# Segment 0 of an infini-attention block: paired projection evictions, work moved to GpSimd, and a new timetable

## The chip, the cores and the metric

The kernel runs on one core of one Trainium2 chip. The metric is device time in microseconds of one execution. A core has five engines with a queue each, worked off strictly in order: TensorE (PE; its weight loads are listed as PEld), VectorE (DVE), ScalarE (ACT), GpSimd (POOL) and SyncE (SP), which here issues nearly all DMAs. Engines wait for one another by semaphores.

## The reference

One sequence of 2048 tokens of 576 channels in bf16, 32 heads of 18 channels, four segments of 512 tokens.

```
x = A_x
h = x + attention(layernorm(x)) @ wo
out = h + gelu(layernorm(h) @ w1 + b1) @ w2 + b2        # 4608 hidden channels

# attention, per head, segments s = 0..3, M = 0, z = 0 at first
a_dot = softmax(qs @ ks.T * scale + mask) @ vs           # within the segment
a_mem = (phi(qs) @ M) / (phi(qs) @ z + 1e-06)            # from the segments before
o     = g * a_mem + (1 - g) * a_dot                      # g = sigmoid(beta), one per head
M, z  = M + phi(ks).T @ vs,  z + sum(phi(ks))            # phi(t) = t + 1 if t > 0 else exp(t)
```

## The kernel before

**Stages.** `build()` describes the work as small operations of one engine each, by segment s: X (layernorm of x and its transpose), P (projections k, q, v), A (attention), M (update of the memory), B (output projection, residual h, second layernorm, transpose), C (first layer of the feed-forward part, F1, and gelu) and D (second layer, F2, and the output). Tokens are handled in tiles of 128 (tl = 0 to 3 in a segment).

**What sets the order.** `TIMETABLE` gives every operation a number and, where a row mixes letters, its engine (p TensorE, a ScalarE, d VectorE, g GpSimd, s SyncE). `schedule` (line 363) sorts all operations by that number and emits them in this order; so the numbers fix each engine's queue, and nothing else is reordered. The cost given to `add` (in us) does not change the order. It serves to pick buffers: `schedule` keeps an estimate of when each buffer of a `Slots` comes free and takes the one that is free first. A key is the stage's tag and the operation's name: `A01val` is the value products of segment 0, query tiles 0 and 1; the n-th entry of a row is the n-th such operation.

**Segment 0's path.** x comes in four tiles. For each, VectorE makes the statistics (`stats`: two BATCH_NORM_STATS2 and an aggregate, lines 669 and 670), GpSimd the reciprocal deviation (`rstd`, 673 and 674) and VectorE the scaled rows (`apply`, 684). Tiles 0 and 1 are only centred (`apply`, 682) and their deviation is multiplied in at the eviction. TensorE transposes (`TX`, 696), ScalarE or VectorE copies the result into xreg (594 or 598). Segments 1 to 3 store the rows and load them back with a transposing DMA (`flip`).

The projections of a tile are 2 x 5 matmuls of 288 columns, one bank of PSUM for each half of the channels. For q and k of tiles 0 and 1 both halves go into one tile of two banks (`proj2`, 750, pool `pr`) and one eviction takes both. All others (`proj`, 740) take one of four single banks `ps_c` for each half and have one eviction each (`copy`, 588). The keys' phi is made of three steps: `ek` (exp, ScalarE 821), `rk` (GpSimd 823) and `fk` (VectorE 825).

Tile 0's q and k are transposed by TensorE (`TQ`, 802), the other tiles' through DRAM (`qkst` and `A0flip`). Scores go into one tile of four banks (`st0`, 913), so each waits for the exp of the one before (ScalarE 916, 1.88 us). The diagonal blocks are masked on VectorE (926) or GpSimd (929), the value products (`val`, 945) are transposed back (`valT`, 959), divided and gated (`rec`, 963 and 964) and written (`comb`, 968).

**The memory.** `M` (849) sums phi(k).T v over the four tiles of a segment, in two halves of the heads. `macc` writes them to MZacc (859, copy in segment 0) or adds them (861). `mblk` (868) makes MZ_blk, the gated block-diagonal form, in four products on GpSimd; it needs MZ_blk zeroed (`memset`), the rows that carry the 1e-6 of the denominator (`eps`: 24 small memsets, 1320 to 1324) and the gates (`gmz`, 1358). Segment 1's `macc` may not change MZacc before segment 0's `mblk` has read it. `A1mem` (1041) is the first that multiplies with MZ_blk; it also needs phi(q) (`eg` ScalarE 1031, `rg` GpSimd 1033, `pq` VectorE 1035).

In segments 1 to 3 the local part of a head group is `valT` (1098), `rec2` (the reciprocal, 1102, and its product with the gate, 1103, both VectorE), `comb` (1106) and `comb2` (1109).

Of the kernel before, what the change touches and what calls it, by code (L numbers as in the profile page):

```python
# [11 lines left out]
ACT = mybir.ActivationFunctionType  # L12
# [12 lines left out]
    "A00exp": "a 89 106",  # L25
    "A00mask": "g 98 142 156 118",
    "A00st0": "p 82 101",
    "A01comb": "g 188 167 215 229",
    "A01exp": "a 124 140 160 176",
    "A01mask": "g136 d143 g180 g172",  # L30
    "A01oT": "d 228 233 230 236 235",
    "A01rec": "d 178 161 212 224",
    "A01st0": "p 119 137 155 170",
    "A01val": "p 149 200",
    "A01valT": "d 175 157 208 221",
    "A02comb": "g 294 347",
    "A02exp": "a 193 227 210 245 263 282 296",
    "A02mask": "g251 g238 g259 d309",
    "A02rec": "d 289 341",
    "A02st0": "p 189 223 207 242 260 276 291",  # L40
    "A02val": "p 255 279 313 315",
    "A02valT": "d 284 319",
    "A03comb": "g 408 449",
    "A03exp": "a 317 348 330 364 382 395 415",
    "A03mask": "g 353 365 370 428",
    "A03oT": "d 371 484 442 486 496",
    "A03rec": "d 386 445",
    "A03st0": "p 310 344 325 360 372 392 410",
    "A03val": "p 376 381 434 437",
    "A03valT": "d 385 440",  # L50
    "A0flip": "s 90 80 111 129 151 158 203 252",
    "A0opad": "g 127",
    "A1comb": "g534 g605 g630 g677 d714 g748 g790 d814",
    "A1comb2": "g541 g609 g636 g695 g731 g760 d798 d816",
    "A1eg": "a 390 377 472 542 650 680 683 741",
    "A1exp": "a 443 480 463 527 495 550 569 587 603 624 643 672 657 693 719 709 749 762 778 736",
    "A1flip": "s 352 340 414 477 520 516 615 645",
    "A1mask": "g444 g488 g492 g493 g497 g549 g526 d544 g563 g586 d600 g598 d631 g619 g641 g642 g674 g688 g697 g681 g664 g699 g725 d726 d769 d763 g768 d770 "
        "d774 g788 g764 g742",
    "A1mem": "p 458 471 606 607 662 735 708 756",  # L60
    "A1memT": "d 465 475 611 622 673 738 712 766",
    "A1memfin": "g538 g568 g625 g684 g723 d755 g751 g804",
    "A1oT": "d 678 707 782 819 821",
    "A1pq": "d 416 417 589 575 658 694 687 750",
    "A1rec": "d 467 482 621 676 706 739 718 785",
    "A1rec2": "d 532 579 628 675 713 743 789 812",
    "A1rg": "g 401 397 558 548 594 581 668 705",
    "A1st": "p 432 474 461 518 490 545 566 582 599 617 638 667 652 689 715 704 744 758 771 730",
    "A1val": "p 519 560 613 649 698 733 773 794",
    "A1valT": "d 530 573 623 654 711 740 779 807",  # L70
    "A2comb": "d931 d949 g983 g1014 g1053 d1072 g1126 d1157",
    "A2comb2": "g933 g964 g990 d1017 d1057 g1076 g1141 g1159",
    "A2eg": "a 732 837 903 935 948 956 1031 1055",
    "A2exp": "a 842 813 857 829 890 927 941 911 975 960 987 1011 1025 999 1045 1064 1074 1100 1087 1135",
    "A2flip": "s 671 783 808 864 850 889 1030 992",
    "A2mask": "d873 g862 g825 d868 g881 g855 g910 d908 g947 d950 d955 g958 d988 d986 g995 d982 d1028 d1027 g1020 d1033 g1032 g1006 d1050 g1049 g1094 g1079 "
        "d1109 g1106 g1131 d1095 g1146 d1147",
    "A2mem": "p 809 915 932 951 998 1009 1085 1078",
    "A2memT": "d 822 921 973 962 1001 1026 1090 1092",
    "A2memfin": "g909 g929 d977 g1010 d1021 g1060 g1133 g1128",  # L80
    "A2oT": "d 991 1052 1127 1165 1164",
    "A2pq": "d 800 904 928 945 994 1003 1062 1069",
    "A2rec": "d 866 926 976 969 1019 1043 1104 1102",
    "A2rec2": "d 901 943 981 1008 1047 1071 1124 1156",
    "A2rg": "g 754 878 916 937 874 952 1056 1065",
    "A2st": "p 839 797 853 826 875 923 938 905 972 953 984 1007 1022 997 1036 1058 1070 1096 1083 1120",
    "A2val": "p 877 919 970 996 1041 1063 1117 1151",
    "A2valT": "d 882 939 979 1005 1046 1068 1121 1155",
    "A3comb": "g1209 d1290 d1345 g1360 g1398 d1417 g1446 d1469",
    "A3comb2": "g1245 g1299 d1347 d1367 d1406 d1422 d1454 d1470",  # L90
    "A3eg": "a 1145 1178 1247 1304 1261 1337 1351 1396",
    "A3exp": "a 1152 1163 1171 1231 1184 1264 1277 1255 1309 1295 1344 1326 1357 1369 1389 1402 1412 1426 1440 1451",
    "A3flip": "s 1042 1093 1123 1099 1189 1276 1205 1334",
    "A3mask": "g1193 d1172 d1198 d1186 g1213 d1249 d1243 g1214 d1271 g1283 g1297 g1284 g1332 g1321 g1319 g1313 d1352 g1341 g1338 g1373 g1366 g1386 d1404 "
        "d1397 g1408 d1430 g1420 g1433 g1436 g1461 g1459 d1460",
    "A3mem": "p 1211 1268 1259 1343 1294 1361 1400 1414",
    "A3memT": "d 1217 1275 1280 1349 1305 1371 1415 1429",
    "A3memfin": "d1244 d1289 g1327 g1363 g1370 g1377 d1445 d1453",
    "A3oT": "d 1323 1424 1438 1474 1471",
    "A3pq": "d 1149 1215 1256 1317 1265 1340 1392 1401",  # L100
    "A3rec": "d 1234 1288 1285 1354 1328 1376 1427 1452",
    "A3rec2": "d 1206 1287 1324 1358 1395 1413 1444 1468",
    "A3rg": "g 1116 1114 1154 1310 1251 1308 1380 1383",
    "A3st": "p 1148 1160 1167 1197 1180 1262 1272 1252 1306 1292 1342 1322 1353 1365 1382 1399 1409 1421 1437 1447",
    "A3val": "p 1199 1260 1301 1339 1384 1407 1439 1462",
    "A3valT": "d 1203 1263 1316 1356 1394 1410 1443 1466",
    "B00Po": "p 244 248",
    "B00T": "p 299 307",
    "B00apply": "d 273",
    "B00copy": "d303 a312",  # L110
    "B00dma": "s 201 720",
    "B00hadd": "d 250 254",
    "B00rstd": "g 266",
    "B00stats": "d 256",
    "B00tail": "g 281",
    "B01Po": "p 262 267",
    "B01T": "p 301 308",
    "B01apply": "d 293",
    "B01copy": "d 305 314",
    "B01dma": "s 211 450",  # L120
    "B01hadd": "d 268 271",
    "B01rstd": "g 285",
    "B01stats": "d 277",
    "B01tail": "g 298",
    "B02Po": "p 503 523",
    "B02apply": "d 585",
    "B02dma": "s 452 793 592",
    "B02hadd": "d 508 528",
    "B02rstd": "g 571",
    "B02stats": "d 562",  # L130
    "B02tail": "g 590",
    "B03Po": "p 502 509",
    "B03apply": "d 543",
    "B03dma": "s 405 806 564",
    "B03flip": "s 635 626",
    "B03hadd": "d 512 514",
    "B03rstd": "g 522",
    "B03stats": "d 517",
    "B03tail": "g 556",
    "B1Po": "p 888 851 828 831 848 871 835 833",  # L140
    "B1apply": "d 918 860 900 856",
    "B1dma": "s 847 959 922 791 1139 887 838 954 912 792 849 865",
    "B1flip": "s 936 971",
    "B1hadd": "d 893 894 832 834 870 876 841 844",
    "B1rstd": "g 899 843 892 852",
    "B1stats": "d 896 836 884 846",
    "B1tail": "d920 d885 g906 d858",
    "B2Po": "p 1174 1176 1204 1216 1228 1223 1173 1170",
    "B2apply": "d 1229 1311 1278 1232",
    "B2dma": "s 1098 1238 1250 1182 1282 1318 1196 1431 1293 1091 1179 1237",  # L150
    "B2flip": "s 1336 1364",
    "B2hadd": "d 1183 1185 1208 1221 1239 1242 1175 1177",
    "B2rstd": "g 1226 1303 1273 1227",
    "B2stats": "d 1220 1225 1266 1187",
    "B2tail": "d1246 d1315 g1291 g1235",
    "B3Po": "p 1493 1490 1483 1481 1559 1561 1476 1479",
    "B3apply": "d 1549 1535 1570 1528",
    "B3dma": "s 1485 1498 1553 1423 1512 1540 1543 1618 1583 1428 1587 1531",
    "B3flip": "s 1593 1604",
    "B3hadd": "d 1495 1496 1488 1489 1560 1562 1480 1482",  # L160
    "B3rstd": "g 1548 1534 1568 1504",
    "B3stats": "d 1500 1497 1563 1484",
    "B3tail": "d1552 d1537 g1575 d1529",
    "C00F1": "p 329 318 346 383 366 413 446 438 481",
    "C00copy": "a336 d337 a327 d331 d363 d358 d407 d394 d375 d380 d424 d427 d460 d457 d447 d453 d491 d499",
    "C00dma": "s 173 217 261 326 335 359 374 398 423",
    "C00gelu": "a 422 505",
    "C01F1": "p 692 670 679 710 717 737 747 765 784",
    "C01copy": "d702 a701 d686 d685 d696 d691 d722 d721 a728 d729 d746 d753 d759 a757 d772 d786 d795 d803",
    "C01dma": "s 682 690 700 716 727 745",  # L170
    "C01gelu": "a 787 867",
# [1279 lines left out]
```

## Time and profile before

| what | us |
|---|---|
| three runs: median (lowest, highest) | 452.2 (448.96, 452.28) |
| the profiled execution | 450.67 |
| its span, first to last instruction | 449.0 |
| TensorE busy | 439.1 |
| VectorE busy | 292.0 |
| ScalarE busy | 298.9 |
| GpSimd busy | 180.2 |

The page gives each engine's busy time with its share of the span, the span in 40 slices (a digit is a share in tenths; PEclk is TensorE's granted clock in tenths of full speed), the chain of work that ended last, and groups of instructions by line. Other views list instructions in order of time (start, length, engine, line, output<-input), sum busy time by stretch, or say for whom an engine waited. A group's line reads: busy us, mean ns of one, then the engine's idle time before them and what ended it. TensorE's matmuls overlap, so its busy time also counts what a matmul needs to drain.

### The profile page before, as it was taken

The numbers are of one execution on the slowest core, as the hardware profiler recorded it, in microseconds if no ns is written. First come the engines' busy times: TensorE is split into PE (matmuls) and PEld (weight loads), VectorE is DVE, ScalarE is ACT, GpSimd is POOL, SyncE is SP. The second block draws the span as 40 slices with busy tenths as digits, with TensorE's granted clock in tenths as the row PEclk, the third lists the DMA queues.
The fourth block names the chain that finished last, engine by engine and source line by source line (L and its number), as shares of the span: only waits on it lengthen the run. The fifth ranks groups of instructions, "written<-read, shape, count | busy, mean of one in ns | idle before, by whom it ended". The sixth has DMA issues, their size and how long they took to land.

```text
span 449.0 us, 11498 instructions
## 1 busy us (share of the span) xinstructions
PE 439.1 (98%) x4815; PEld 280.3 (62%) x4815; DVE 292.0 (65%) x623; ACT 298.9 (67%) x267; POOL 180.2 (40%) x304
## 2 busy tenths in 40 slices
PE   8979999899999999999999999999999999999997
PEld 4756677566677677664344766645447875445775
DVE  6899896689888879887788877887675111000120
ACT  4879998799878879768899977674665002664000
POOL 6596667538874546744351437621201010000000
PEclk9989999899999999999999999999999999999999
DMA  7999989697788977874772925603552681640110
GB/s 267 235 236 251 255 212 293 195 251 234 181 214 279 295 252 177 234 110 117 199 214 77 216 88 130 142 36 108 154 175 73 169 241 24 213 161 1 39 42 26
DMA packets 81588, 76.54 MB, mean 170 GB/s; under 512 B 59008, under 2 KB 68736, under 8 KB 81536
## 3 DMA queue, kind: packets, MB, share of 16 engines
q1 hardware_dynamic: 81392, 75.66, 63.4%
q8 instruction: 37, 0.61, 0.5%
q10 hardware_dynamic: 144, 0.15, 0.1%
q14 instruction: 15, 0.12, 0.1%
HBM read 42.63 MB, written 19.20 MB: 138 GB/s over the span
## 4 chain that ended last, share of the span: by engine, by line
PE 92%; DVE 3%; POOL 2%; DMA 1%; issue 1%; ACT 0%; POOLq 0%
PE ps_c L1290 32%; PE ps_c L1203 16%; PE ps_c L747 16%; PE ps_l L1203 8%; PE ps_c L1240 7%; PE st L1064 4%; PE ps_c L1090 4%; PE ps_c L1041 1%; PE pr L758 1%; PE ps_c L849 1%; PE st L913 1%; DVE ln L669 1%; PE ps_c L945 1%; POOL MZ_blk L1324 1%; DMA x<-in_A_x_dram 1%
## 5 line engine op out<-in xcount | busy, mean ns | idle before, releaser
L1068 ACT ACTIVATE pt<-st 128x2048 bf16<-128x2048 f32 x60 | 112.6, 1877 | 34.9 <-PE st L1064 29.0
L1290 PEld LDWEIGHTS <-hT 128*128 128x128 bf16 x1152 | 110.7, 98 | 33.9 <-issue 5.7
L1203 PEld LDWEIGHTS <-w1g 64*128 64x128 bf16 x972 | 46.6, 94 | 56.5 <-issue 3.4
L1290 PE MATMUL ps_c<-w_lo,hT 128*128 128x288 bf16 x576 | 78.0, 286 | 0.0
L1290 PE MATMUL ps_c<-w,hT 128*128 128x288 bf16 x576 | 77.9, 286 | 0.0
L1203 PE MATMUL ps_c<-xreg,w1g 64*128 64x512 bf16 x648 | 72.9, 376 | 0.0
L747 PE MATMUL ps_c<-hT,xreg 128*128 128x288 bf16 (+1 forms) x440 | 62.6, 291 | 0.2
L1079 POOL TENSOR_SCALAR_AFFINE_SELECT pt<-pt 128x512 bf16<-128x512 bf16 x62 | 44.1, 720 | 44.7 <-ACT pt L1068 44.7
L1302 DVE TENSOR_TENSOR ot<-ps_c,hc 128x288 bf16<-128x288 f32 x32 | 14.1, 450 | 69.6 <-PE ps_c L1290 69.2
L1208 ACT ACTIVATE hT<-ps_l,b_col 128x512 bf16<-128x512 f32 x36 | 22.7, 685 | 46.8 <-PE ps_l L1203 46.8
L747 PEld LDWEIGHTS <-xreg 128*128 128x128 bf16 (+1 forms) x440 | 41.1, 99 | 15.9 <-issue 4.7
L1218 DVE TENSOR_SCALAR hT<-ps_c,b_col 128x512 bf16<-128x512 f32 x48 | 34.5, 743 | 13.8 <-PE ps_c L1203 13.6
L916 ACT ACTIVATE pt<-st 128x2048 bf16<-128x2048 f32 x20 | 37.6, 1879 | 3.2 <-PE st L913 2.4
L1240 PE MATMUL ps_c<-xreg,w1g 64*128 64x256 bf16 x648 | 38.1, 270 | 0.0
L1203 PE MATMUL ps_l<-xreg,w1g 64*128 64x512 bf16 x324 | 35.1, 376 | 0.0
L1240 PEld LDWEIGHTS <-w1g 64*128 64x128 bf16 x648 | 30.2, 94 | 6.7 <-issue 2.9
L673 POOL TENSOR_SCALAR ln<-ln 128x1 f32<-128x1 f32 x32 | 8.3, 259 | 64.4 <-DVE ln L670 62.5
L1223 ACT ACTIVATE hT<-hT 128x8192 bf16<-128x8192 bf16 (+2 forms) x6 | 31.8, 5321 | 0.3 <-DVE hT L1218 0.2
L1216 ACT ACTIVATE hT<-ps_c,b_col 128x512 bf16<-128x512 f32 x24 | 16.0, 685 | 16.3 <-PE ps_c L1203 16.1
L1064 PE MATMUL st<-qk 32*128 32x512 bf16 (+3 forms) x384 | 24.0, 303 | 0.0
L1251 DVE TENSOR_TENSOR hT<-ps_c,b_col 128x512 bf16<-128x512 f32 x31 | 20.6, 680 | 5.0 <-PE ps_c L1240 4.0
L747 PE MATMUL ps_c<-wt_o,oT 128*128 128x288 bf16 x160 | 22.5, 286 | 0.0
(111 smaller groups left out, 579.4 us busy)
## 6 DMA issues: line engine op xcount, KB each, us to landing
w1g<-in_B_w_dram SPq DMA_DIRECT2D x42, 576.0 KB, 4.9
qkd<-qk_pad SPq DMA_DIRECT2D x15, 512.0 KB, 3.8
hd<-h SPq DMA_DIRECT2D x16, 288.0 KB, 3.8
hc<-hd SPq DMA_DIRECT2D x16, 288.0 KB, 4.3
w_lo<-in_B_w_dram SPq DMA_DIRECT2D x3, 864.0 KB, 6.3
w<-in_B_w_dram SPq DMA_DIRECT2D x3, 864.0 KB, 9.7
xb<-in_A_x_dram SPq DMA_DIRECT2D x16, 144.0 KB, 4.2
x2d<-xn SPq DMA_DIRECT2D x14, 160.0 KB, 1.8
```

What stands on the lines that cost most here:

```text
L747: nc.tensor.matmul(out=c.t[:, 0:HALF], lhsT=xTb.t[0:kk, k, ts], rhs=wt[0:kk, hf, k, :], start=(k == 0), stop=(k == 4))
L916: ex = add(ps, {"act": 1.88}, lambda e: nc.scalar.activation(out=pt.t[:], in_=st.t[:], func=ACT.Exp, scale=scale), [sc], pt, [st], table=" ...
L1064: nc.tensor.matmul(out=st.t[:, i, off:off + n_], lhsT=qk[rows, 1, kt * P:(kt + 1) * P], rhs=qk[rows, 0, kt * P:L], start=True, stop=True, ...
L1068: ex = add(ps, {"act": 1.88}, lambda e, st=st, pt=pt: nc.scalar.activation(out=pt.t[:], in_=st.t[:], func=ACT.Exp, scale=scale), [sc], pt, ...
L1079: nc.gpsimd.affine_select(out=blk, in_=blk, pattern=[[0, 4], [1, P]], compare_op=ALU.is_ge, fill=0.0, base=0, channel_multiplier=-1)
L1203: nc.tensor.matmul(out=cc[w].t[:], lhsT=w1.t[rows, k, q, :], rhs=x2T[s].t[rows, k, :], start=(k == 0), stop=(k == ND - 1))
L1208: ready_f[f + w] = [add(pf - 12, {"act": 0.68}, lambda e, f=f, w=w, cc=cc: nc.scalar.activation(out=hT[:, :, f + w, :], in_=cc[w].t[:].rea ...
L1218: nc.vector.tensor_scalar(out=dst, in0=src, scalar1=b, scalar2=None, op0=ALU.add)
L1223: ge = add(2.9, {"act": 0.40 * (f1 - f0) + 0.25}, lambda e, f0=f0, f1=f1: nc.scalar.activation(out=hT[:, :, f0:f1, :], in_=hT[:, :, f0:f1, ...
L1240: nc.tensor.matmul(out=cc[w].t[:, q * 2 * P:(q + 1) * 2 * P], lhsT=w1.t[rows, k, q, :], rhs=x2T[s].t[rows, k, ts], start=(k == 0), stop=(k ...
L1251: nc.vector.tensor_tensor(out=dst, in0=src, in1=b.unsqueeze(2).to_broadcast([P, 2, 2 * P]), op=ALU.add)
L1290: nc.tensor.matmul(out=c.t[:, 0:HALF], lhsT=hT[:, tl // 2, f, (tl % 2) * P:(tl % 2 + 1) * P], rhs=w2_c[ch][:, f - ch * WCH, hf * HALF:(hf ...
```

## The change

- In segment 0 all projections use `proj2`: q and k of tiles 2 and 3 and v of all four tiles go into two adjacent banks and have one eviction. For that the four banks `ps_c` become one tile, of which `Slots` gives out single banks or an even pair. Q and k of tiles 0 and 1 stay in `pr`.
- `apply` may run on GpSimd where it is not the centring of tiles 0 and 1. The timetable puts 24 there: one of segment 0's x, three, four and three of segments 1 to 3, and thirteen of the second layernorm.
- The product with the local gate becomes an operation of its own (`gate`) on VectorE or GpSimd (12 of 24).
- The 24 memsets of `eps` become eight operations of three.
- Two `ones` move from ScalarE to GpSimd (as memsets).
- The costs given to `add` change, and the whole timetable is new.

```diff
-    "A00exp": "a 89 106",
-    "A00st0": "p 82 101",
-    "A01mask": "g136 d143 g180 g172",
-    "A01val": "p 149 200",
-    "A1mem": "p 458 471 606 607 662 735 708 756",
-    "B02dma": "s 452 793 592",
-    "B3dma": "s 1485 1498 1553 1423 1512 1540 1543 1618 1583 1428 1587 1531",
-    "M0M": "p 162 159",
-    "M0mblk": "g 411",
-    "M1M": "p 402 421",
-    "M1macc": "d 419 429",
-    "X1apply": "d 73 79 126 120",
-    "X2apply": "d 183 165 264 206",
-    "eps": "g 384",
...
+    "A00exp": "a 91 70",
+    "A00st0": "p 86 68",
+    "A01mask": "d128 d110 g143 g142",
+    "A01val": "p 129 171",
+    "A1gate": "g492 d579 g615 d679 g705 d747 g780 d799",
+    "A1mem": "p 395 479 516 607 631 720 695 757",
+    "B02dma": "s 353 818 597",
+    "B3dma": "s 1511 1520 1555 1452 1579 1582 1585 1636 1594 1454 1764 1584",
+    "M0M": "p 162 135",
+    "M0mblk": "g 391",
+    "M1M": "p 405 386",
+    "M1macc": "d 413 392",
+    "X1apply": "g79 g75 g122 d95",
+    "X2apply": "g 156 177 277 313",
+    "eps": "g 187 336 390 322 331 330 335 334",
...
+    def pick(self, t0):
+        free = self.home.free
+        if self.mate is not None:
+            return self.mate.n + 1
+        if self.lead:
+            return min(range(0, len(free), 2), key=lambda i: max(free[i], free[i + 1]))
+        if hasattr(self.home, "whole"):
+            return min(range(len(free)), key=lambda i: (free[i] >= INF, free[i ^ 1] < INF, max(free[i], t0), -free[i ^ 1]))
+        return min(range(len(free)), key=lambda i: free[i]) if self.want is None else self.want
...
+    PAIRED = (0,)
...
-    c_s = slots(4, [P, 512], "ps_c", F32, psum)
+    c_all = psum.tile([P, 4, 512], F32, name="ps_c")
+    c_s = Slots([c_all[:, j, :] for j in range(4)])
+    c_s.whole = c_all
+
+    def two_banks():
+        a = Buf(c_s, lead=True)
+        return a, Buf(c_s, mate=a)
...
-            return add(prio, {"dve": dcost}, apply, [a, b if centred is None else None] + list(extra), dst_buf, [sm, xsrc], name="apply")
+            return add(prio, {"dve": dcost} if centred is not None else {"dve": dcost, "pool": 0.72 if dcost < 0.7 else 0.95}, apply, [a, b if centred is None else None] + list(extra), dst_buf, [sm, xsrc], name="apply")
...
+                if s in PAIRED:
+                    banks = two_banks()
+                    a = proj2(PE_P[s] + 0.001 * tl if s > 1 else p0 + (0.6 if s == 0 else 0), xT, tl, "v", [xn_ok[s, tl]], lambda c=banks[0]: c.t2, banks)
+                    v_ok[s, tl, 0] = v_ok[s, tl, 1] = copy(p0 - 0.5, 0.66, 0.76, lambda tl=tl: v_augs[s][tl][:, :, 0:Dh].rearrange("p (a h) d -> p a h d", a=2),
...
                 def c0(e, g=g, r1=r1, t1=t1):
                     nc.vector.reciprocal(out=r1.t[:], in_=t1.t[:, :, Dh])
-                    nc.vector.tensor_scalar(out=r1.t[:], in0=r1.t[:], scalar1=omg_q[:, g:g + 1], scalar2=None, op0=ALU.mult)
+
+                def cg(e, g=g, r1=r1):
+                    VEC[e].tensor_scalar(out=r1.t[:], in0=r1.t[:], scalar1=omg_q[:, g:g + 1], scalar2=None, op0=ALU.mult)
...
-        def eps_fn(e):
-            for t in MZ_blk[:2]:
-                for i in range(4):
-                    for n in (2, 1, 0):
-                        VEC[e].memset(t[32 * i:32 * i + Dh + 1 + n, :, 32 * i + Dh:32 * i + Dh + 1], eps_parts[n])
+        def eps_fn(e, t, i):
+            for n in (2, 1, 0):
+                VEC[e].memset(t[32 * i:32 * i + Dh + 1 + n, :, 32 * i + Dh:32 * i + Dh + 1], eps_parts[n])
...
-        z_eps = [add(3.55, {"pool": 2.6}, eps_fn, begin + later_mz, name="eps")]
+        z_eps = [add(3.55, {"pool": 0.56}, lambda e, t=t, i=i: eps_fn(e, t, i), begin + [later_mz[j]], name="eps") for j, t in enumerate(MZ_blk[:2]) for i in range(4)]
```

More of the change, by code (lines that the diff above doesn't have):

```diff
@@ L670, in stats @@
                 nc.vector.bn_aggr(out=sm.t[:, 12:14], in_=sm.t[:, 0:12].rearrange("p (a b) -> p a b", b=6))
-            a = add(prio, {"dve": 1.10}, stats, after, sm, [xsrc], name="stats")
+            a = add(prio, {"dve": 1.06}, stats, after, sm, [xsrc], name="stats")
             def rstd(e):
@@ L748, in proj, with proj2 @@
             return add(prio, {"pe": 0.62}, fn, list(after) + w_ok[nm], c, [xTb], name="P" + nm)
-        def proj2(prio, xTb, tl, nm, after, c):
+        def proj2(prio, xTb, tl, nm, after, out, banks):
             ts = slice(tl * P, (tl + 1) * P)
@@ L757, in fn @@
                         kk = KTAIL if k == 4 else P
-                        nc.tensor.matmul(out=c.t[:, hf, 0:HALF], lhsT=xTb.t[0:kk, k, ts], rhs=wt[0:kk, hf, k, :],
+                        nc.tensor.matmul(out=out()[:, hf, 0:HALF], lhsT=xTb.t[0:kk, k, ts], rhs=wt[0:kk, hf, k, :],
                                          start=(k == 0), stop=(k == 4))
-            return add(prio, {"pe": 1.24}, fn, list(after) + w_ok[nm], c, [xTb], name="P" + nm)
+            return add(prio, {"pe": 1.24}, fn, list(after) + w_ok[nm], list(banks), [xTb], name="P" + nm)
         fk_bufs, v_ok, qk_st, v0_read, mz_read = {}, {}, {}, [], {}
@@ L930, in mask @@
                                                     base=0, channel_multiplier=-1)
-                    masks[u] = add(ps, {"dve": 0.70, "pool": 1.15}, mask, [ex, tri_ok], None, [pt], name="mask")
+                    masks[u] = add(ps, {"dve": 0.87, "pool": 1.14}, mask, [ex, tri_ok], None, [pt], name="mask")
                     masks[u].bias = {"dve": MASK_BIAS}
@@ L1080, in mask @@
                                                     base=0, channel_multiplier=-1)
-                    mk = add(ps, {"dve": 0.54, "pool": 0.72}, mask, [ex] + later, None, [pt], name="mask")
+                    mk = add(ps, {"dve": 0.46, "pool": 0.68}, mask, [ex] + later, None, [pt], name="mask")
                     mk.bias = {"dve": MASK_BIAS}
@@ L1335, in build, with ones_fn @@
         gr.tag = ""
[L1336 to L1338 removed]
+        def ones_fn(e, t):
+            if e == "act":
+                nc.scalar.activation(out=t[:, :, :, Dh:Dh + 1], in_=ident[:].rearrange("p (a b c) -> p a b c", a=TPS, c=1), func=ACT.Copy, scale=0.0, bias=1.0)
+            else:
+                VEC[e].memset(t[:, :, :, Dh:Dh + 1], 1.0)
+        z_va.extend(add(3.5, {"act": 0.8, "pool": 0.3}, lambda e, t=t: ones_fn(e, t), begin + [ident_ok], name="ones") for t in v_all[1:3])
         z_va.append(z_va[0])
@@ L1360, in build @@
         later.append(gates[0])
-        mz_gates = [add(3.55, {"pool": 0.45}, lambda e, i=i: gmz_fn(i), begin + [gates[0]], name="gmz") for i in range(4)]
+        mz_gates = [add(3.55, {"pool": 0.31}, lambda e, i=i: gmz_fn(i), begin + [gates[0]], name="gmz") for i in range(4)]
         w_ok["o"] = load_w(4, "o", 3, begin)
```

55 lines of the change are left out of this document (33 added, 22 removed), and 514 rows, old and new, of the table TIMETABLE.

## The prediction

> **What bounds the kernel now.** I read the busy shares first, then stretches of the span, then TensorE's waits, then the timelines of the two stretches that stand out, and last the row lengths. On the page:
>
> ```profile
> PE 439.1 (98%) x4815; PEld 280.3 (62%) x4815; DVE 292.0 (65%) x623; ACT 298.9 (67%) x267; POOL 180.2 (40%) x304
> ...
> PEclk9989999899999999999999999999999999999999
> ```
>
> TensorE is in work nearly throughout, and the change leaves its 4815 matmuls as they are. So a gain can only come out of TensorE's gaps, its granted clock, or the order of its instructions. Stretches (columns: busy PE, PEld, DVE, ACT, POOL, then PEclk, DMA share, GB/s):
>
> ```profile
> 0.00:20.00 20.00, 18.14 (x150) 11.95 (x150) 14.11 (x38) 13.34 (x22) 10.72 (x30) 1.00 0.86 249
> 20.00:30.00 10.00, 7.69 (x152) 5.10 (x150) 9.63 (x22) 9.02 (x12) 8.69 (x15) 0.97 1.04 229
> 30.00:40.00 10.00, 9.60 (x161) 7.23 (x162) 9.39 (x25) 7.82 (x9) 6.81 (x12) 0.86 1.12 219
> 40.00:70.00 30.00, 30.00 (x461) 21.13 (x460) 25.79 (x62) 27.34 (x35) 20.55 (x34) 1.00 0.95 256
> 70.00:80.00 10.00, 8.08 (x128) 6.00 (x125) 6.28 (x14) 9.20 (x7) 8.32 (x33) 1.00 1.10 278
> 80.00:90.00 10.00, 9.71 (x144) 6.80 (x147) 7.54 (x17) 6.79 (x4) 5.04 (x9) 0.83 0.59 200
> ```
>
> Gaps stand in two places, 20 to 31 us and 77 to 81 us, and behind each the clock falls: 0.03 + 0.14 of 10 us, then 0.17 of 10 us, so 1.7 us lost twice. From 90 us to the tail TensorE has no gap. TensorE's waits name who ended them:
>
> ```profile
> PE ps_c L849 <- DVE MZacc L861: 2.2, 1, 2.2
> PE ps_c L945 <- ACT pt L916: 1.8, 1, 1.8
> PE ps_c L849 <- DVE fk_pad L825: 0.6, 1, 0.6
> ```
>
> The first is at 77.8 us. L861 adds segment 1's memory into MZacc and must wait until GpSimd has read MZacc for MZ_blk (L868). GpSimd's timeline there:
>
> ```profile
> 69.95 4.48 POOL L1324 MEMSET MZ_blk<- 21x8 bf16 x24
> 74.52 1.20 POOL L1033 TENSOR_SCALAR r<-qk 128x512 bf16<-128x512 bf16 x2
> 75.78 0.83 POOL L1358 COPY gmz<-g_bc 32x144 f32<-32x144 f32 x1
> 76.69 0.99 POOL L968 TENSOR_TENSOR o_nat<-t,r 128x288 bf16<-128x288 f32 x1
> 77.64 2.09 POOL L868 TENSOR_TENSOR MZ_blk<-MZacc,gmz 18x152 bf16<-18x152 f32 x4
> ```
>
> The 24 memsets of the 1e-6 rows are one block of 4.48 us, and MZ_blk's four products stand behind it. The other two waits lie at 26 to 30.4 us, in the first value products (A01val) and in M0M:
>
> ```profile
> 28.04 0.57 PE L945 MATMUL ps_c<-pt,v_aug 128*19 128x128 bf16 x28 [1.82 <-ACT pt L916]
> 28.80 0.40 PE L945 MATMUL ps_c<-pt,v_aug 128*19 128x128 bf16 x16 [0.18 <-DVE pt L926]
> ...
> 30.41 0.31 PE L849 MATMUL ps_c<-v_aug,fk_pad 128*128 128x76 bf16 x2 [0.57 <-DVE fk_pad L825]
> ```
>
> Lengths, by shape, of the first 110 us (mean ns of one behind the busy time):
>
> ```profile
> L598 DVE CAST qk_pad<-ps_c 128x288 bf16<-128x288 f32 x21 | 9.2, 450 | 4.1 <-PE ps_c L747 3.7 <-ACT qk_pad L594 0.3
> L594 ACT CAST v_aug<-ps_c 128x288 bf16<-128x288 f32 x9 | 3.6, 397 | 0.6 <-PE ps_c L747 0.4
> L684 DVE TENSOR_SCALAR xn<-x,ln 128x576 bf16<-128x576 bf16 x14 | 8.0, 582 | 1.1 <-POOL ln L674 1.0
> L823 POOL TENSOR_SCALAR rk<-qk_pad 128x576 bf16<-128x576 bf16 x11 | 7.8, 705 | 6.0 <-DVE fk_pad L825 6.0
> L592 ACT ACTIVATE qk_pad<-pr,ln 128x576 bf16<-128x576 f32 x3 | 2.2, 742 | 2.0 <-PE pr L758 1.9
> L596 DVE TENSOR_SCALAR qk_pad<-pr,ln 128x576 bf16<-128x576 f32 x1 | 0.8, 803 | 0.0
> ```
>
> **The change part by part.** I go against the profiled execution: 450.67 us, span 449.0. It lies 1.5 us under the median of the three runs (452.2) and inside them (448.96 to 452.28), so its result is set against both.
>
> *Order of TensorE.* Sorting TensorE's entries by their numbers gives 213 changes between whole-array and row- or column-tiled instructions before, 205 after. Start to start, a 288-column matmul takes 0.122 us, and 0.218 to 0.220 when a score follows, so about 0.1 a change: 8 x 0.1 = **-0.8**.
>
> *Two banks, one eviction.* Eight pairs of evictions become eight of 576 elements. ScalarE: 2 x 0.40 against 0.74; VectorE: 2 x 0.45 against 0.80. That is 0.06 to 0.10 each, 0.7 us over both engines and all eight, none of it on TensorE. Against it the first half now waits for the second (0.61 us of matmuls), and a pair holds two of four banks until one eviction ends. Both go into the next step.
>
> *First stretch, to M0M.* TensorE's work ahead of A01val is the same in both orders (23.2 us with the warm-up, by start-to-start lengths), so what counts is ScalarE and VectorE. After the change the first scores need the transposed keys that VectorE now copies (P00copy.3, behind fk and two stats): about 16.5 us, where the first scores started at 16.64 before. From there ScalarE has exp 1.88, copy 0.74, ek 0.68, exp 1.88, copy 0.74, gates 0.27, exp 1.88, ek 0.68, exp 1.88 = 10.6, less some 0.1 of overlap for each: it ends at 27.5 to 28.2, as 27.99 before. Then VectorE: two masks (0.69 to 1.58 in its rows), two evictions of 0.80 and fk 0.74 put M0M near 30.4, where it really began before (30.41). Gaps of TensorE before: 0.21 + 1.84 + 0.20 + 0.61 = 2.9, and 1.7 of clock. After: between 2.0 (ScalarE never late) and 5.0 (each bank pair also waits); I take 3.4, the tally along that chain, and half of the 1.7 us of clock (0.7), since the gaps are shorter but more. **-4.6 + 4.1 = -0.5.**
>
> The clock's fall is seen behind unbroken gaps of 1.8 and 2.3 us. The Trainium skill, page "TensorE: Matmul & The Clock Gate", section "Part 1: The HAM clock gate", says half rate comes after an idle window of some 3.4 us; the trace does not agree as to length (2.3 us sufficed). By the page no gap that I forecast would cost clock, and the sum would be 1.0 us lower.
>
> *The 1e-6 rows and GpSimd's queue to MZ_blk.* Eight operations of three memsets are 4.48/8 = 0.56 each, and in the new order only one (eps 390) stands right in front of MZ_blk (391). But GpSimd gets eight applies of x and two of h in front of it. Price on GpSimd: no row of this operation; nearest is L823, same shape, 0.67 at its shortest; not below 0.43 (VectorE's median for L684), not above 1.35 (GpSimd's 576-element f32 add, L1276). I take 0.72 for x, 0.95 for h (f32 input). Summed by rows, GpSimd's work through M0mblk is 53.7 before and 59.8 after (10 applies +7.7, two ones +0.6, rk +0.7, one rstd fewer -0.8, three products fewer -2.0). Before it ended at 79.7, so GpSimd stood waiting 26 us: 9.3 in the first 20 us, 15 to 17 later. TensorE's work ahead of the first user: before 69.6 ahead of the second M1M, reached at 77.9; after 66.9 ahead of A1mem, which now comes earlier (A1mem 395 right behind M1M 386). Start and gaps put 8.3 us on that before (77.9 - 69.6), so 7.5 now, and TensorE is there at 74.4. MZ_blk is done by then if GpSimd waits no more than 14.6, of which 9.3 are the first 20 us. Fewer waits are likely, because the new queue has work where the old one waited (3.3 us at 57, waiting for L823's input). Bounds: 0 lost, and 10.0 (waits as before: 59.8 + 9.3 + 15.3 = 84.4). I take 2.0, near the low end, because following the queue from 23 us on I find it nearly always backed up and ending at 72 to 76, with small waits of TensorE for late masks on the way; and 0.3 of clock. Behind the wait stand, on VectorE, M1macc and A1's memory, and on TensorE all of P2. Gone is 2.28 + 0.36 + 1.7 = 4.3. **-4.3 + 2.3 = -2.0.**
>
> *Later.* VectorE loses 24 applies (0.43 x, 0.58 h) and 12 gate products (0.25) to GpSimd, and the new order has it nearer to its masks at one place: summed rows ahead of A1val.3 leave 3.7 us to TensorE's sum, 7.5 before. Between 0 and 2: **+0.6**. GpSimd's gate product is not shown: 0.22 (L673) to 0.67 (L968), and a hop each way; hidden, as only the transposes of o wait. The two "ones" leave ScalarE (0.75 each); GpSimd 0.11 to 0.95, taken 0.3.
>
> *SyncE's queue.* An x load for B02 now stands between A1's first two transposing loads and waits for A02comb; about 5 us of room to A1's second rg. Segment 3's last store of h (B3dma 1764) and its load back (1765) move behind an output store: 3.8 + 4.3 us of landing and 1.35 for the add of b2, about 10, under 24 F2 steps of 0.735 = 17.6. Cost 0; without that cover 10.
>
> **Sum:** 450.67 - 0.8 - 0.5 - 2.0 + 0.6 = 448.0, 0.9% under the median 452.2.
>
> **Rivals.**
> 1. *Both gaps really go.* First stretch at its low bound without loss of clock (-2.6), MZ_blk in time (-4.3), -0.8: 450.7 - 7.7 = **443.0**. For it: GpSimd's 26 us of waiting. Against: the chain of exps is no shorter.
> 2. *GpSimd's applies hold up VectorE.* In the trace VectorE's L684 at 22.69 took 1.45 instead of 0.43, beside a GpSimd mask from 22.61. Some 15 applies before A1val.3, at half of that 1.0, make 7.5, less the 3.7 of room: 448.0 + 3.8 = **451.8**. Against: most of VectorE's rows are at their shortest. The Trainium skill, page "SBUF — State Buffer", section "Who interferes with whom", says that the pair of ports which both share is locked for a whole instruction; the trace agrees (1.45 against 0.43).
> 3. *Slower: GpSimd late at MZ_blk.* If it waits as before, it ends at 84.4, TensorE stands 10.0 us at A1mem, with 1.7 of clock: 448.0 - 2.3 + 11.7 = **457.4**. It decides against the change (1% over the median, 456.7) when MZ_blk ends after 83.7 us. For it: the waits of GpSimd are on other engines, which the change does not speed up. Against: the work now waiting in its queue.
>
> **How the numbers follow.** Forecast 0.38 (own range 446 to 450), rival 1 0.30, rival 2 0.18, rival 3 0.14. About 1% is what a measurement of this kernel can tell from no change (its three runs span 0.7%). Under 447.7: rival 1 and a third of the forecast, 0.42; over 456.7: 0.14; between: 0.44. The range from 442 to 456.5 takes in rivals 1 and 2 and leaves out rival 3.
>
> **What would show it.** TensorE's waits: no L861 at 77 us, but one of 1 to 4 us at A1mem (L1041's row) ended by MZ_blk; if none, rival 1. M0M near 30 us again, and the 30 to 40 us clock between 0.86 and 1. GpSimd's apply 0.65 to 0.8. The eps memsets in groups of three of 0.56. VectorE's fk and mask rows over 1 us by the dozen would be rival 2. A new gap of TensorE after 130 us would make my sum wrong.

## The result and the profile after

The changed kernel takes 727.4 us (median of 6 runs, 721.0 to 734.9) against 451.0 (6 runs, 449.0 to 452.3) for the kernel before: 1.609 times as long, 95% interval 1.605 to 1.614. That ratio is of the fast runs alone and leaves out the one of 734.9 us. The profiled execution took 726.9 us, its span is 725.1. The forecast was 448.0 with a range up to 456.5; no rival of the prediction comes near.

The page of the kernel after, its busy times and TensorE's granted clock:

```profile
PE 517.2 (71%) x4808; PEld 315.1 (43%) x4815; DVE 274.2 (38%) x592; ACT 295.8 (41%) x259; POOL 230.4 (32%) x336
...
PEclk9955889795887978999968999999988789999999
```

TensorE was busy for 98% of the span, and now for 71%. No other engine has taken its place: VectorE, ScalarE and GpSimd are at 38, 41 and 32%. So nothing is the bound by its amount of work; the engines wait for one another. The lower clock adds to it (mean 0.875, before 0.992). A kernel that waits everywhere is read by its waits. Three of the kernel after (us in all, times, longest):

```profile
ACT hT L1258 <- DVE hT L1260: 37.7, 8, 15.0
...
DVE hT L1260 <- ACT hT L1258: 26.0, 7, 6.9
...
PE ps_c L1245 <- DVE hT L1260: 19.8, 10, 3.1
```

L1258 and L1260 are the evictions of the first feed-forward layer (F1) on ScalarE and on VectorE. They read different banks and write different parts of hT, and yet each waits for the other. Before, ScalarE's same line (L1216) waited 16.3 us, of it 16.1 for TensorE's matmuls:

```profile
L1216 ACT ACTIVATE hT<-ps_c,b_col 128x512 bf16<-128x512 f32 x24 | 16.0, 685 | 16.3 <-PE ps_c L1203 16.1
```

TensorE's timeline at M0M and the first projection of segment 1 (start, length, in brackets the wait before):

```profile
40.51 0.28 PE L888 MATMUL ps_c<-v_aug,fk_pad 128*128 128x76 bf16 x2 [0.53 <-DVE v_aug L624]
...
45.89 1.36 PE L773 MATMUL ps_c<-hT,xreg 128*128 128x288 bf16 x5 [3.65 <-DVE MZacc L898]
```

M0M starts at 40.5 us, where I expected 30.4. The projection has its inputs (TensorE loaded a first block of xreg for it at 42.0 us), but it stands 3.65 us behind VectorE's copy of the memory out of ps_c. GpSimd's applies are also far over what I priced:

```profile
L710 POOL TENSOR_SCALAR xn<-x,ln 128x576 bf16<-128x576 bf16 x11 | 26.0, 2366 | 0.8
```

One takes 2.37 us on average (2.31 the median), where my upper bound was 1.35.

So there were two suspects, and a third to be excluded. **Theory 1:** the four banks ps_c are now one tile, and an access to one bank waits for earlier accesses of other engines to the others; TensorE can't run ahead into a free bank. **Theory 2:** 24 applies of 2.31 us make GpSimd late for everything. **Theory 3:** the paired evictions or the new order do it.

### The profile page after: what moved, and what is told of

It is laid out like the page before. It is cut to its first block, busy times and chain, and to the rows that moved or that the text cites. A ratio compares the mean times of both kernels' runs of the same rounds, so it can differ in the third digit from the quotient of the medians.

```text
span 725.1 us, 11462 instructions
## 1 busy us (share of the span) xinstructions
PE 517.2 (71%) x4808; PEld 315.1 (43%) x4815; DVE 274.2 (38%) x592; ACT 295.8 (41%) x259; POOL 230.4 (32%) x336
## 5 line engine op out<-in xcount | busy, mean ns | idle before, releaser
L1332 PEld LDWEIGHTS <-hT 128*128 128x128 bf16 x1152 | 115.1, 101 | 81.4 <-issue 43.4
L1245 PE MATMUL ps_c<-xreg,w1g 64*128 64x512 bf16 x648 | 92.5, 440 | 41.4 <-DVE hT L1260 19.8
L1245 PEld LDWEIGHTS <-w1g 64*128 64x128 bf16 x972 | 55.4, 102 | 110.0 <-issue 70.3
L1332 PE MATMUL ps_c<-w_lo,hT 128*128 128x288 bf16 x576 | 86.0, 303 | 20.6 <-DVE ot L1344 8.1
L773 PE MATMUL ps_c<-hT,xreg 128*128 128x288 bf16 (+1 forms) x360 | 70.7, 353 | 37.0 <-DVE v_aug L624 8.7
L1118 POOL TENSOR_SCALAR_AFFINE_SELECT pt<-pt 128x512 bf16<-128x512 bf16 x55 | 36.9, 682 | 87.5 <-ACT pt L1107 87.5
L1260 DVE TENSOR_SCALAR hT<-ps_c,b_col 128x512 bf16<-128x512 f32 x49 | 34.9, 747 | 76.0 <-PE ps_c L1245 50.1
L1282 PE MATMUL ps_c<-xreg,w1g 64*128 64x256 bf16 x648 | 45.7, 301 | 20.0 <-ACT hT L1291 6.4
L1258 ACT ACTIVATE hT<-ps_c,b_col 128x512 bf16<-128x512 f32 x23 | 15.2, 685 | 89.1 <-DVE hT L1260 37.7
L1282 PEld LDWEIGHTS <-w1g 64*128 64x128 bf16 x648 | 38.0, 104 | 26.9 <-issue 23.4
L773 PE MATMUL ps_c<-wt_o,oT 128*128 128x288 bf16 x160 | 27.4, 320 | 15.5 <-ACT hT L1258 5.0
L1318 POOL TENSOR_TENSOR hc<-hc,b_bc 128x576 f32<-128x576 f32 x8 | 10.8, 1360 | 85.7 <-DMA hc<-hd 85.7
L1129 PE MATMUL ps_c<-pt,v_aug 128*19 128x512 bf16 (+3 forms) x384 | 19.5, 330 | 19.8 <-DVE hT L1260 10.9
```

The costliest lines, as they stand in the source:

```text
L773: nc.tensor.matmul(out=c.t[:, 0:HALF], lhsT=xTb.t[0:kk, k, ts], rhs=wt[0:kk, hf, k, :], start=(k == 0), stop=(k == 4))
L1118: nc.gpsimd.affine_select(out=blk, in_=blk, pattern=[[0, 4], [1, P]], compare_op=ALU.is_ge, fill=0.0, base=0, channel_multiplier=-1)
L1129: nc.tensor.matmul(out=ox[g].t[32 * i:32 * i + Dh + 1, kt * P:L], lhsT=va[kt][:, 4 * g + i, :], rhs=pt.t[:, i, off:off + n_], start=kt == ...
L1245: nc.tensor.matmul(out=cc[w].t[:], lhsT=w1.t[rows, k, q, :], rhs=x2T[s].t[rows, k, :], start=(k == 0), stop=(k == ND - 1))
L1258: nc.scalar.activation(out=dst, in_=src, func=ACT.Identity, bias=b)
L1260: nc.vector.tensor_scalar(out=dst, in0=src, scalar1=b, scalar2=None, op0=ALU.add)
```

## The experiments

The kernel before, run beside each, had medians of 450.5 to 450.9 us.

| run | us | to before (95%) |
|---|---|---|
| before, ps_c one tile | 722.9 | 2 runs, 716.7 and 729.2 |
| before, 24 applies on GpSimd | 481.6 | 1.071 (1.067 to 1.076) |
| after, four tiles, no pairs | 472.5 | 1.051 (1.046 to 1.055) |
| after, all applies on VectorE | 731.9 | 1.626 (1.618 to 1.634) |
| before, two tiles of two banks | 509.0 | 1.130 (1.127 to 1.134) |
| after, VectorE applies, two tiles, pairs | 537.7 | 1.193 (1.189 to 1.197) |
| the same without pairs, first free bank | 579.3 | 1.286 (1.272 to 1.301) |
| the same with pairs, first free bank | 576.6 | 1.280 (1.270 to 1.291) |
| after, four tiles, VectorE applies | 451.6 | 1.0025 (1.0012 to 1.0039) |
| before, forms of the apply | 478.8 | one run |
| after, four tiles, GpSimd add and multiply | 456.7 | 1.014 (1.011 to 1.016) |
| the same, first four applies on VectorE | 451.6 | 1.0021 (1.0003 to 1.0039) |
| before, 1e-6 rows early | 447.4 | 0.994 (0.992 to 0.996) |

**One tile, nothing else.** The kernel before with this edit:

```diff
-    c_s = slots(4, [P, 512], "ps_c", F32, psum)
+    c_all = psum.tile([P, 4, 512], F32, name="ps_c")
+    c_s = Slots([c_all[:, j, :] for j in range(4)])
```

> The kernel before, with one edit: the four banks ps_c are views of one tile of four banks instead of four tiles. Order, engines and instructions are those of before. Theory 1 (the common tile makes an access to any of its banks wait for earlier accesses to the others, so TensorE can no longer run ahead into a free bank): this edit alone brings most of the 276 us, 600 to 730 us, with ScalarE's F1 evictions (L1249 and its neighbour) waiting for VectorE's and the granted clock under 0.92. Theory 2 (GpSimd's applies of 2.31 us delay everything) and theory 3 (the paired evictions or the new timetable do): no change, 448 to 455 us.

Measured: 716.7 and 729.2 us. This edit alone costs 266 us by the faster run, which is also the profiled one, and 279 by the other; the whole change cost 276. The page and, from the groups, ScalarE's F1 evictions (busy, mean ns, then its idle time and what ended it):

```profile
PE 516.3 (72%) x4815; PEld 309.7 (43%) x4815; DVE 295.0 (41%) x623; ACT 299.9 (42%) x267; POOL 174.1 (24%) x304
...
L1217 ACT ACTIVATE hT<-ps_c,b_col 128x512 bf16<-128x512 f32 x24 | 15.9, 686 | 87.8 <-DVE hT L1219 46.4
```

The evictions last as long as before (0.69 us); only the idle time ahead of them has grown, from 16.3 to 87.8 us, and over half of it ends with VectorE's F1 eviction. One hand-over in the middle, TensorE, then ScalarE, then VectorE:

```profile
245.59 0.39 PE L1065 MATMUL st<-qk 32*128 32x512 bf16 x4
247.33 0.58 PE L1042 MATMUL ps_c<-e,MZ_blk 128*128 128x512 bf16 x1 [1.34 <-DVE hT L1252]
```

```profile
245.71 0.84 ACT L1250 ACTIVATE hT<-ps_c,b_col 128x256 bf16<-128x256 f32 x2 [5.95 <-PE ps_c L1091]
```

```profile
246.58 0.69 DVE L1252 TENSOR_TENSOR hT<-ps_c,b_col 128x512 bf16<-128x512 f32 x1 [1.70 <-ACT hT L1250]
```

VectorE starts when ScalarE ends (246.55), and TensorE starts when VectorE ends (247.27): read them in order of time and it is one queue through three engines. The compiled program says the same without any time. In its list of instructions, two of the first F1 evictions on ScalarE, as they are in before and with one tile (each names the semaphore that it waits for; a semaphore is named after the engine that raises it):

```
63 L1249 Activation hT<-ps_c1_137,b_col 128x256 [waits PE_49]
66 L1249 Activation hT<-ps_c3_139,b_col 128x256 [waits PE_49]
...
63 L1250 Activation hT<-ps_c_136,b_col 128x256 [waits DVE_49]
66 L1250 Activation hT<-ps_c_136,b_col 128x256 [waits DVE_49]
```

The two read banks 1 and 3. With one tile, the values that they wait for are raised by VectorE's transposing read of bank 2 (L960) and by its F1 eviction of bank 0 (L1252): a read of one bank waits for a read of another.

The list as a whole has fewer waiting instructions on TensorE (614 before, 504 with one tile, 442 after), but one that waits for ps_c now waits for the whole tile. TensorE waits 163.5 us for VectorE in 189 stretches and 29.6 for ScalarE in 28, against 4.8 in 5 and 1.8 in one. Its span is 198.7 us idle and 516.3 busy, against 9.9 and 439.1: of the 266 us of span, 189 are gaps, and 77 are longer busy time, at a mean clock of 0.897.

The Trainium skill, page "PSUM — Partial Sum Buffer", section "PSUM bank collisions raise a hardware error", says that two engines clash on one bank, and that accesses to different banks run clean. The trace of before agrees: of ScalarE's 34 F1 evictions out of ps_c (L1216 and L1249), 19 run at the same time as one of VectorE's 79 out of another bank (L1218 and L1251). With one tile none of the 34 does. So these waits come from how the program names its banks; the memory does not ask for them.

**The applies, in both directions.** On the kernel before the 24 go to GpSimd, and on the kernel after all go to VectorE (one of the rows each):

```diff
-    "X1apply": "d 73 79 126 120",
+    "X1apply": "g73 g79 g126 d120",
...
```

```diff
-    "X1apply": "g79 g75 g122 d95",
+    "X1apply": "d79 d75 d122 d95",
...
```

> The kernel before, with the same 24 applies on GpSimd as after (the n-th entry of each row gets the engine that it has after; numbers stay). Theory 2: most of the loss, over 600 us. Theory 1: little of it. Each apply costs GpSimd 2.31 us instead of nothing, ten of them before MZ_blk, which is done at 79.7 us in before; GpSimd has about 26 us of waiting there to take up part of 23 us, so TensorE would stand 0 to 23 us longer at the first user of MZ_blk, plus a few us behind each applied row: 452 to 480 us.

> The kernel after, with all 38 applies on VectorE; the common tile, the pairs and the new timetable stay. Theory 1: 680 to 725 us, since the waits on the common tile stay. Theory 2: 445 to 470 us.

Measured: 481.6, just over the top of the range, and 731.9, 7 us over the range. Alone the applies cost 31 us; TensorE then stands 4.6 us for MZacc at 98 us and 3.0 for an applied row at 65 us:

```profile
65.51 0.61 PE L696 MATMUL ps_c<-ident,xn 128*128 128x128 bf16 x4 [3.02 <-POOL xn L684]
...
98.44 1.17 PE L849 MATMUL ps_c<-v_aug,fk_pad 128*128 128x76 bf16 x16 [4.63 <-DVE MZacc L861]
```

Beside the common tile, taking them back gains nothing (731.9 against 727.4). Theory 2 falls as the main cause. The two losses don't add up. A likely reason, not tried by itself, is that GpSimd (busy for 32% of the kernel after) has time while the other engines wait in one queue.

**Four tiles in the kernel after.** `c_s = slots(4, ...)` again, each pair split into two operations that follow one another:

```diff
-    "P01Pv": "p 115 52",
+    "P01Pv": "p115 p115.5 p52 p52.5",
...
-    PAIRED = (0,)
+    PAIRED = ()
```

> The kernel after, with the four banks ps_c as four tiles again, which also undoes the eight pairs in ps_c (each pair is two projections and two evictions that follow one another directly at the pair's place). The applies stay on GpSimd, the new timetable, the gate product, the eps in eight and the ones stay. Theory 1: the loss is nearly gone, 452 to 480 us. Theory 2: still over 600 us. Theory 3 for the timetable: still over 600 us; theory 3 for the paired evictions: as theory 1, so this run does not tell these two apart, but the first one (one tile, no pair) does.

> The kernel after, with the four banks ps_c as four tiles again (the pairs undone as well) and all applies on VectorE. What is left of the change: the new timetable, the gate product by itself, the 1e-6 rows in eight operations, two ones on GpSimd. Theory 1 with theory 2 for the small rest: the applies cost the 22 us by which the kernel with four tiles lies over before, so the time falls back to 443 to 454 us. Theory 3 for the timetable: it stays over 460 us, because the new order has a loss of its own that the kernel with four tiles also held.

Measured: 472.5, so 255 of the 276 us are gone, and with the applies on VectorE as well 451.6, 0.25% over before. The new order has no great loss of its own; nor has it a gain. As the main cause theory 3 falls for the order; for the pairs it fell with the first run, which has none in ps_c.

**Two tiles of two banks.**

> The kernel before, with the banks ps_c as two tiles of two banks each; order, engines and instructions as before. Theory 1: a false wait remains only between the two banks of one tile, so the time lies clearly between 450.6 (four tiles) and 722.9 (one tile): 500 to 620 us. A rival that the loss comes from the address of a bank inside a larger tile, or from anything else that a view of a tile brings: as with one tile, over 700 us.

> The kernel after with all applies on VectorE and the eight pairs kept, but with the four banks as two tiles of two banks, a pair being one whole tile. The kernel with four tiles, no pairs and applies on VectorE took 451.6; before with two tiles took 509.0, 58 us over before. Theory 1, with pairs that cost nothing by themselves: 451.6 + 58, so 495 to 520 us, since a pair has only true waits and eight of the false ones go. Theory 3 (a pair costs much by itself): over 525 us. Pairs that pay: under 495 us.

> The kernel after with all applies on VectorE, the pairs undone, and the banks as two tiles of two, given out as in before (the bank that is free first). Against the run with pairs in two tiles (537.7, which was 28 us over before with two tiles, 509.0) it takes away the pairs and the rule that puts single banks into a tile already in use. Theory 1 with that rule or the pairs as the cause of the 28 us: 500 to 518 us. If the new order itself suffers more from two tiles than the old one: 525 to 545 us.

> The kernel after with all applies on VectorE, the pairs kept as whole tiles, the banks as two tiles of two, but single banks given out as in before (the one that is free first) instead of beside a bank in use. The rule that puts two single banks into one tile makes just those banks neighbours that are in use together, which is what theory 1 makes dear: if it is the cause of the 28 us, 500 to 518 us. If the pairs are (theory 3): 525 to 545 us, as with the rule.

Measured: 509.0 for before, as theory 1 said; the rival (a view costs something by itself) falls. After took 537.7 with pairs, and here my expectations missed: by the first I had to suspect the pairs or the rule in `pick` that puts a single bank beside one in use. Without both the time rose to 579.3, and with pairs but without the rule to 576.6. So the pairs change nothing (the intervals overlap), the rule gains 39 us, and the new order, with the small changes that go with it, bears two-bank tiles worse than the old (128 us over its own four-tile time, against 58). Why the rule helps was not tried; it would fit theory 1 if two crowded banks in one tile leave the other tile free, but that is only argued, and so what the rule and the order do with two-bank tiles stays open.

**What is dear in GpSimd's apply.** One kernel with five forms of it:

> The kernel before with 24 applies on GpSimd, of which some are computed otherwise, to see what makes 2.31 us of them: segment 1's rows only subtract the mean (one scalar per partition), segment 2's rows use two constants, the second layernorm of segment 1 uses one scalar per partition and one constant, that of segment 2 two scalars per partition with multiply and add instead of subtract and multiply; the others are as in the change. The output is therefore not the reference's in these rows. If the scalars per partition cost the time: constants 0.65 to 0.75 us (as rk), one scalar 1.3 to 1.6, two 2.3 in either order of operations. If the subtraction costs it: constants 2.3 as well, and multiply and add 0.7.

```profile
L696 POOL TENSOR_SCALAR xn<-x,ln 128x576 bf16<-128x576 bf16 x4 | 9.7, 2432 | 0.1
L692 POOL TENSOR_SCALAR xn<-h,ln 128x576 bf16<-128x576 f32 x4 | 8.9, 2222 | 0.0
L690 POOL TENSOR_SCALAR xn<-x 128x576 bf16<-128x576 bf16 x4 | 8.6, 2154 | 0.3
L688 POOL TENSOR_SCALAR xn<-x,ln 128x576 bf16<-128x576 bf16 x3 | 5.3, 1753 | 0.0
L694 POOL TENSOR_SCALAR xn<-h,ln 128x576 bf16<-128x576 f32 x4 | 3.3, 819 | 0.1
```

From the top: subtract and multiply by two scalars per partition (2.43), by one scalar and a constant (2.22), by two constants (2.15), subtract alone (1.75), and last multiply and add by two scalars per partition: 0.82. The scalars are not what costs, the subtraction is. (The last row reads f32 and three of the others bf16, but that is not the reason: in the next kernel the same addition and multiplication take 0.82 from bf16 too.) The Trainium skill, page "GPSIMD Engine Reference", section "3.1 Elementwise — side-by-side cycle accounting", gives 1.8 cycles of 1.2 GHz for an element at best; for 576 that is an estimate of 0.86 us. Multiply and add come out at about that (0.82), the forms with a subtraction do not.

**The change as I had priced it.** Four tiles, and GpSimd negates the mean first:

```diff
+                if e == "pool":
+                    nc.gpsimd.tensor_scalar(out=sm.t[:, 16:17], in0=sm.t[:, 12:13], scalar1=-1.0, scalar2=None, op0=ALU.mult)
+                    nc.gpsimd.tensor_scalar(out=dst_buf.t[:, 0:D], in0=src(), scalar1=sm.t[:, 16:17], scalar2=sm.t[:, 15:16], op0=ALU.add, op1=ALU.mult)
+                    return
```

> The kernel after with the two costs taken away that the runs have named: the banks ps_c are four tiles (pairs undone), and GpSimd's applies negate the mean first (one 128x1 instruction of about 0.22 us) and then add and multiply, which took 0.82 us for h where subtract and multiply took 2.30. All 24 stay on GpSimd, and timetable, gate, eps in eight and ones are those of the change. This is the change as the prediction priced it (0.72 for x, 0.95 for h). If the other terms of the prediction were right: 446 to 450 us, with no wait of TensorE for MZ_blk over 2.3 us. If the new order loses what the kernel with the applies on VectorE lost too (451.6): 450 to 454 us. If GpSimd is still the bound, because it has 24 times 1.0 us more than before and is late with masks and keys: over 456 us.

Measured: 456.7, the case in which GpSimd is still late. GpSimd, then VectorE, then TensorE:

```profile
18.77 0.82 POOL L710 TENSOR_SCALAR xn<-x,ln 128x576 bf16<-128x576 bf16 x1
19.67 0.67 POOL L857 TENSOR_SCALAR rk<-qk_pad 128x576 bf16<-128x576 bf16 x1
```

```profile
20.37 0.76 DVE L859 SCALAR_TENSOR_TENSOR fk_pad<-ek,rk 128x576 bf16<-128x576 bf16 x1 [3.50 <-POOL rk L857]
```

```profile
22.48 1.39 PE L775 MATMUL ps_c<-hT,xreg 128*128 128x288 bf16 x10 [1.63 <-DVE qk_pad L622]
...
33.77 1.07 PE L890 MATMUL ps_c<-v_aug,fk_pad 128*128 128x76 bf16 x14 [1.70 <-DVE fk_pad L859]
```

Three applies stand before GpSimd's second rk, the one for the keys of tile 1 (13.8 to 19.6 us). VectorE stands 3.5 us at fk, and behind fk in its queue are a set of statistics and two evictions; TensorE waits for these. A fourth apply (30.5 us) stands before the rk that M0M needs. To test this, only these four went back:

> The kernel with four tiles and GpSimd's applies as add and multiply (456.7 us), with the four applies of the tiles 2 and 3 of segment 0 and of segment 1's first rows (X01 and X1, four of 24 on GpSimd) back on VectorE. In the trace of that kernel three of them stand before GpSimd's first rk of the second key pair, and VectorE waited 3.5 us for it at 20.4 us, TensorE 1.6 us at 22.5; a fourth stands before the rk that M0M waited 1.7 us for at 33.8, and the granted clock was 0.66 in 30 to 40 us. If these four are the cause of the 5 us over the kernel with all applies on VectorE (451.6): 449 to 452.5 us, with M0M near 30 us. If the other twenty are: 455 to 457 us.

Measured: 451.6. The stretch of 30 to 40 us (PE, PEld, DVE, ACT, POOL, clock, DMA, GB/s), with the four on GpSimd and on VectorE, and M0M in the latter:

```profile
30.00:40.00 10.00, 7.82 (x121) 5.71 (x121) 8.44 (x16) 5.12 (x6) 7.47 (x12) 0.66 0.96 205
```

```profile
30.00:40.00 10.00, 9.10 (x166) 6.96 (x167) 9.65 (x27) 8.82 (x10) 8.25 (x13) 1.00 1.19 266
```

```profile
30.22 0.66 PE L890 MATMUL ps_c<-v_aug,fk_pad 128*128 128x76 bf16 x14 [0.64 <-DVE fk_pad L859]
```

M0M has its fk at 30.2 us instead of 33.8, and no clock is lost. The four cost 5.1 us; the other twenty on GpSimd cost nothing that the runs can tell (451.6 with them and without).

**One part that pays.** The kernel before, with the 1e-6 rows in eight operations at places where GpSimd stood waiting (one zeroing of MZ_blk moves up with them, from 332 to 303):

```diff
-    "eps": "g 384",
+    "eps": "g 335 336 366 367 299 300 301 302",
```

> The kernel before, with the 1e-6 rows in eight operations of three memsets (as in the change) and these at places of the timetable where GpSimd stood waiting before: 299 to 302 and, with the zeroing of that MZ_blk moved up to 303, 335, 336, 366 and 367. GpSimd has 3.3 us of waiting near 54 us, 1.1 near 61 and 1.2 near 67. By the prediction's term for this step MZ_blk is done 4.4 us sooner, the gap of TensorE at 77 us and its clock loss go, and the time falls by 3 to 4.3 us to 446 to 448 us. If another wait follows at once behind it: less than 1 us, over 449.5 us.

Measured: 447.4 us, 0.994 of before (0.992 to 0.996): the only version here that beats both kernels, by 3.1 us. GpSimd's timeline, then the stretch of 70 to 90 us before and here:

```profile
53.73 2.09 POOL L1322 MEMSET MZ_blk<- 21x8 bf16 x12
...
72.21 2.15 POOL L868 TENSOR_TENSOR MZ_blk<-MZacc,gmz 18x152 bf16<-18x152 f32 x4
```

```profile
70.00:90.00 20.00, 17.79 (x272) 12.80 (x272) 13.82 (x30) 15.99 (x10) 13.36 (x41) 0.91 0.85 239
```

```profile
70.00:90.00 20.00, 19.74 (x307) 14.47 (x305) 17.64 (x36) 19.17 (x14) 10.91 (x19) 1.00 1.06 268
```

MZ_blk's products end at 74.4 us instead of 79.7. TensorE's gap there goes (2.0 us of busy time more) and so does the loss of clock (0.09 of 20 us, 1.8).

## Why the prediction was wrong

**The step that failed** is the one on two banks with one eviction. I priced the evictions ("none of it on TensorE") and the time for which a pair holds two of four banks. That the four banks become one tile stood in the diff and in my own description of it, and it got no price and no bounds: a term of 0 where the runs show 266 us or more. It was just the case for bounds, since I had no row of before for what a common tile costs. The pairs, to which I gave the attention, are innocent (with two tiles of two banks 576.6 with them, 579.3 without). Their evictions take 0.64 us on ScalarE and 0.71 to 0.81 on VectorE; I had 0.74 and 0.80.

**GpSimd's apply** was mis-sized: 0.72 and 0.95 from the row of rk, bounds 0.43 to 1.35, measured 2.31. I took the row of the same shape and engine, but of other operations in the instruction. The 24 cost 31 us on the kernel before; on the after with four tiles the form alone costs 16 (472.5 to 456.7). Rival 3, GpSimd late at MZ_blk, had the right mechanism for that: with the applies on the kernel before, TensorE stood 4.6 us there.

**First stretch, -0.5.** It failed too, in one place. I wrote that "what counts is ScalarE and VectorE", and did not put the moved applies into the queue ahead of rk. With the four applies on VectorE, M0M has its fk at 30.2 us, where I said 30.4, with no clock lost in 20 to 40 us, where I had half of 1.7; with them on GpSimd at 1.06 us it has it at 33.8. That 30.2 meets 30.4 is in part luck. In that kernel ScalarE's chain came in the order that I wrote, but I had added it up too long: from first scores at 16.65 us it ended at 27.2, not at 27.5 to 28.2. And the fk itself then took 1.55 us instead of 0.74, beside a mask on GpSimd (28.46 to 29.55).

**The 1e-6 rows and MZ_blk, -2.0.** The first half is right: what was gone I put at 4.3, and moving these rows alone gives 3.1. One operation of three takes 0.49 to 0.54 us, I had 0.56. The second half was too hopeful about GpSimd: with the priced change MZ_blk is done at 81.2 us, not at 72 to 76. TensorE does not wait for it, because it comes to A1mem only at 81.8 us, where I had 74.4; the delay has moved ahead of it:

```profile
79.10 2.08 POOL L909 TENSOR_TENSOR MZ_blk<-MZacc,gmz 18x152 bf16<-18x152 f32 x4
```

```profile
81.79 0.38 PE L1082 MATMUL ps_c<-e,MZ_blk 128*128 128x512 bf16 x1
```

**Order, -0.8, and later, +0.6.** The first is not seen by itself. In the after with four tiles and applies on VectorE, TensorE's gaps up to 130 us and its lost clock come to 9.0 us (before 10.2), but the span is 0.2 us longer, so there is no gain of the order to be found. After 130 us TensorE's gaps up to the tail come to 1.3 us in the kernel with four tiles and twenty applies on GpSimd, so the second term was about right, and so were the gate product (0.41 us mean, bounds 0.22 to 0.67) and the ones (0.66, bounds 0.11 to 0.95).

**Rivals.** The sign of rival 2 is absent in the kernel after: fk takes 0.74 us and VectorE's masks of segments 1 to 3 take 0.49 on average, not over 1. Rivals 1 and 3 set TensorE's two gaps against each other, and neither holds a gap that recurs all through the kernel; all three were variations of my own sum, and none asked what the new tile does. The sign that I had named for a wrong sum is there: from 130 to 700 us TensorE stands idle for 160 us.

**Sum.** With the common tile and the dear subtraction out of the way the change is worth +5.7 us as it stands, and about +0.8 with four applies moved, where I had -2.7. So the rest of the working was off by 8.4 us, and by 3.5 with the four moved.

## What to carry to other kernels

When a diff makes several buffers views of one tile, read it as a change of what waits for what, ahead of any duration: look in the instruction list whether engines that worked on different buffers now wait for each other, and give the merger a price or bounds. Price an instruction on another engine from a row with the same operation, and not only the same shape; and put every moved instruction into the queue ahead of each thing that others wait for. Where a block of small set-up work stands in front of a late product, put its pieces where that engine idles: it was the one part of this change that paid.

## What the runs showed of the hardware

- GpSimd took 1.75 to 2.43 us for 576 elements with a subtraction, and 0.82 with multiply and add on the same two scalars per partition (0.88 to 0.95 on average in the kernel with four tiles). Adding a negated mean costs 0.24 us (median; 0.29 on average) more for the negation and still saves over 1 us.
- In the kernel with one tile the granted clock averages 0.897, with no single wait of TensorE over 2.6 us. The trace's records of the clock show it halved for whole windows of 3.41 us, or several in a row. In the window ahead of each of the 20 falls TensorE's matmuls were busy for 26 to 52%, in one of them with no gap over 0.6 us; in the window ahead of each return, for 83% or more. The Trainium skill, page "TensorE: Matmul & The Clock Gate", section "Part 1: The HAM clock gate", speaks of an idle window of some 3.4 us; here many shorter gaps close together were enough.
- Two losses that both make engines wait did not add up: 266 to 279 us and 31 us apart, 276 us together.
